# Fine factors built one group earlier in a fused attention and feed-forward kernel on one core

## The chip, the core and the metric

The kernel runs on one core of a Trainium2 chip. The time is the device time of one execution in microseconds (us); three executions of the kernel before took 645.56, 646.25 and 647.49 us, so the median is 646.25 us.

The engines go by the names of the profile: PE multiplies matrices (PEld is its loading of weights), DVE is the vector engine, ACT the scalar engine, POOL the third element-wise engine, which in this kernel mostly issues transfers, and SP only issues transfers. Each engine works through its own list of instructions in a fixed order, and an instruction that waits for a semaphore holds everything behind it on that engine.

## The reference, cut to what matters

```python
# q, k, v: (4 batches, 8 heads, 768 positions, 64), lam: one decay per head, blocks of 64
for b in range(nb):
    intra = ((qb @ kb^T) * Dmask) @ vb              # inside the block, decay lam ** distance
    inter = (qb * lam_pow) @ kv_state               # from everything before it
    out[:, :, sl] = intra + inter
    kv_state = lam_block * kv_state + (kb * rev_pow)^T @ vb
x = attn_out.transpose(0, 2, 1, 3).reshape(3072, 512)
h = x @ w_in                                        # 512 -> 2048
g = h - np.tanh(h)
return g @ w_out                                    # 2048 -> 512
```

All of it is float32. The two large products with `w_in` and `w_out` are most of the arithmetic.

## The kernel before, in words

**Groups and stages.** The 3072 rows are worked in six groups of 512 (128 positions of each of the four batches), numbered 0 to 5; `g` is the group. In each group the attention makes a 512 x 512 block of `x` (tiles `xt`), `up` (from L702) multiplies it with `w_in` in four units `u` of 512 columns, `shrink` takes `h - tanh(h)`, and `down` and `down_twice` multiply the result (tiles `g11`, `g12`, `g21`, `g22` and `gS1`, all shown as `g` or `gS`) with `w_out`. While the units and products of group g run, the attention of group g+1 is woven in between by the function `pieces`, whose names `P2`, `P4`, `P5`, `P6` say after which product a part comes.

**Seven products in place of eight.** Every large product is done by a scheme with seven half-size products in place of eight, numbered 1 to 7, with sums of the operands before and sums of the results after. From group 1 on most of the seven are split a second time in the same way (`down_twice`, matmuls of 128 x 128 by 128 x 128 at L1015); before such a product `sums_twice` makes two new tiles `s1`, `s2` on DVE and a sum in place (L983 to L992). `down_twice` takes the seven small products in the order 1, 2, 6, 5, 7, 3, 4: the third of them (product 6) is the first that reads `s2`, the fourth reads `s1`, and the sixth (product 3) reads a tile from which `s2` has been subtracted after the second small product.

**Factors.** The sums of the `w_out` side don't depend on the group. They are made once and kept in DRAM: `factors` holds the first level, `fine` the second. PE reads them as pieces of 256 KB (tile `wb`), which POOL's queue loads into a ring of eight buffers (`piece`, L875 to L900); a buffer is loaded again when PE has read the piece in it. Fine factors are needed for products 3 to 7 from group 1 on and for products 1 and 2 only from group 2 on, since group 1 does those two unsplit (`down`, L950). `fine_factors(n)` (L927 to L940) makes the missing ones for product n: four loads of 256 KB of `factors` into tiles `f2` (L934), then four subtractions on DVE (L938, shown as L973, the line of the helper `hold`), each followed by a store of 256 KB to `fine` (L939). Before the change both sets are made in `later_units` of group 2: set 1 during unit 0 and set 2 during units 1 to 3.

**Shared buffers.** The tiles of `fine_factors`, of `inner_weights` (`ws2`, sums of `w_in` that POOL stores to `fine_in` at L785), of `inner_tokens` and of `sums_twice` all come from one pool with four buffers (tag `sums`), handed out in turn. A new tile takes the oldest buffer and waits until its last reader, a store among them, is done.

**What sets the order.** Where the code calls `keep_in_program_order` (directly, or by `hold` and `tied`) the engine's order is that of the code. The loads and stores of `fine_factors` are of this kind among themselves; `hold` fixes DVE's sums. The loads of pieces, the stores of `inner_weights` and the stores of results are placed by the framework's scheduler, which decides where they stand on POOL's queue. Two transfers on POOL's queue are never more than eight places apart in flight: each waits for the landing of the eighth before it.

**Group 1 around the change.** `second_units` (L1304) ends with unit 3, `down(1, 1)` in between; `second_products` (L1281) then has `sums_twice` for product 4, the unsplit `down(1, 2)` (matmuls `w`, L950), part P2 of the attention of group 2, and the split product 4 (`y` and `zw`, L1015). `att_end` (L620) ends an attention with the state products of batches 0, 1 (`P0`) and 2, 3 (`P1`), both in the accumulation bank `yb` (L623 and L626).

Of the kernel before, what the change touches and what calls it, by code (L numbers as in the profile page):

```python
# [18 lines left out]
BLK = 128  # L19
# [5 lines left out]
def kernel(  # L25
# [32 lines left out]
    nc = tc.nc  # L58
# [8 lines left out]
    NU = DFF // 512  # L67
# [29 lines left out]
    HF = BLK // 2  # L97
# [12 lines left out]
    def masks():  # L110
        inj = work.tile([128, BLK], F32, name="inj", tag="qd")
        cross = work.tile([128, 4, 2, HF], F32, name="cross", tag="qd")
        lo, hi = ts(0, HF), ts(1, HF)

        for c in range(HF, BLK, 3):
            nc.gpsimd.memset(inj[hi, c:min(c + 3, BLK)], 0.0)
        nc.gpsimd.tensor_copy(inj[hi, 0:HF], ident[hi, HF:BLK])
        for n in range(4):
            tc.keep_in_program_order(nc.vector.tensor_tensor_scan(
                out=cross[hi, n].rearrange("s c i -> s (c i)"), data0=lam_all[hi, n + 4:n + 5].to_broadcast([HF, BLK]),  # L120
                data1=inj[hi], initial=0.0, op0=AL.mult, op1=AL.add))
        m0 = mask0.rearrange("s j p (c i) -> s p j c i", c=2)
        for q in range(2):
            n = ts(q, 2)
            nc.gpsimd.tensor_copy(mask[lo, n, 0:2], m0[lo, q])
            nc.gpsimd.tensor_copy(mask[lo, n, 2], m0[lo, q + 2, :, 0])
            nc.gpsimd.tensor_copy(mask[hi, n, 1], m0[hi, q, :, 1])
        nc.gpsimd.tensor_copy(mask[hi, :, 0:3:2], cross[hi])
# [86 lines left out]
    SUB = (1, 2, 6, 5, 7, 3, 4)  # L215
    GI = 2
    TWICE = (3, 5, 6, 4, 7, 1, 2)
# [364 lines left out]
    def att_state(g, bs, tag):  # L582
        kv = state_products(g, bs, bank("kv", tag, 4 if tag == "att" else 1))
        st = state[:, bs[0]:bs[0] + 2]
        tied(g == 1, nc.vector.tensor_tensor(st, st, kv, op=AL.add))
# [36 lines left out]
    def att_end(g):  # L622

        if g < NG - 1:
            att_state(g, P0, "yb")
            if g + 1 < NG:  # L626
                att_scores(g + 1, P0)
            att_state(g, P1, "yb")

    def att_sums(g, bs=None):  # L630
        x0, x1 = xt[g, 0], xt[g, 1]
# [145 lines left out]
    def inner_weights(u, ns):  # L777
        for n in ns:
            a11, a12, a21, a22 = (a_quarter(n, u, i, k) for i in range(2) for k in range(2))
            t = late["pool"].tile([128, 4, 128], F32, name="ws2", tag="sums", bufs=4)  # L780
            s1, s2, s4 = (t[:, x] for x in range(3))
            for dst, x, y, op in ((s1, a21, a22, AL.add), (s2, s1, a11, AL.subtract), (a21, a11, a21, AL.subtract),
                                  (s4, a12, s2, AL.subtract)):
                tc.keep_in_program_order(nc.vector.tensor_tensor(dst, x, y, op=op))
            nc.gpsimd.dma_start(out=fine_in[INNER.index(n)].rearrange("x p u c -> p u x c")[:, u], in_=t[:, 0:3])  # L785
# [53 lines left out]
    RING = 2 * B  # L839
# [24 lines left out]
    stream = [x for g in range(1, NG) for x in pieces_of(g)]  # L864
    sent = {"n": 0}

    first_blk = next(i for i, x in enumerate(stream) if x[0] == NG - 1)

    def ring(i):
# [3 lines left out]
    def piece(g, n, x):  # L873

        i = stream.index((g, n, x))  # L875
        while sent["n"] < len(stream):
            r = ring(sent["n"])
            mine = [at_ for at_ in range(first_blk if r == "blk" else 0, sent["n"] + 1) if ring(at_) == r]
            if r == "wb" and sum(at_ >= i for at_ in mine) > RING:
                break  # L880
            if r == "blk" and len(mine) % 2 == 1 and len(mine) > 8 and mine[-8] >= i:
                break
            g_, n_, x_ = stream[sent["n"]]
            if r == "wb":
                t = late["pool"].tile([128, 2, 256], F32, name="wb", tag=r, bufs=RING)
            else:
                if len(mine) % 2 == 1:
                    sent["pair"] = late[r].tile([128, 2, 2, 256], F32, name="wb", tag=r)
                t = sent["pair"][:, 1 - len(mine) % 2]
            if isinstance(n_, tuple):  # L890
                nc.gpsimd.dma_start(out=t.rearrange("p m c -> p (m c)"), in_=fine_in[  # L891
                    INNER.index(n_[1]), (5, 6, 3).index(x_)].rearrange("p u c -> p (u c)"))
            elif twice(g_, n_):
                nc.gpsimd.dma_start(out=t.rearrange("p m c -> p (m c)"),  # L894
                                    in_=fine[TWICE.index(n_), SLOT.index(x_)].rearrange("p u c -> p (u c)"))
            else:
                nc.gpsimd.dma_start(out=t, in_=factors[XAT[FACT[n_][1]]][:, 2 * x_:2 * x_ + 2, :])
            blks[stream[sent["n"]]] = t
            sent["n"] += 1
        return blks.pop((g, n, x))  # L900
# [12 lines left out]
    def sums_once(g, dst, x, y):  # L913

        for u in (0, 2):
            tc.keep_in_program_order(nc.vector.tensor_tensor(
                hidden(g, dst)[:, u:u + 2], hidden(g, x)[:, u:u + 2], hidden(g, y)[:, u:u + 2], op=AL.subtract))
# [57 lines left out]
    def sums_twice(g, n, whole=True):  # L975
        a11, a12, a21, a22 = quarter(g, n)
        s1, s2 = (late["pool"].tile([128, NU, 128], F32, name=f"s{x}", tag="sums", bufs=4) for x in (1, 2))
        hold(s1, a21, a22, op=AL.add)
        hold(s2, s1, a11, op=AL.subtract)
        low[g, n] = (s1, s2)  # L980
        if whole:
            sum_third(g, n)
# [75 lines left out]
    def every(product):  # L1058
        for _ in product:
            pass  # L1060

    def steps(product, n):
        for _ in range(n):
            next(product)
# [214 lines left out]
        run(table.get(at_, ()) if g < NG - 1 else ())  # L1279

    def second_products(g):  # L1281
        sums_twice(g, 4)
        sums_once(g, 11, "S1", 11)
        every(down(g, 2))
        pieces(g, "P2")
        pieces(g, "P4")
        sums_twice(g, 5)
        product = down_twice(g, 4)
        steps(product, 4)
        sums_once(g, 21, 21, 11)  # L1290
        sums_twice(g, 6)
        every(product)
        product = down_twice(g, 5)
        steps(product, 2)
        pieces(g, "P5")
        sums_twice(g, 7)
        every(product)
        product = down_twice(g, 6)
        steps(product, 2)
        sums_twice(g, 3)  # L1300
        every(product)
        pieces(g, "P6")
        every(down_twice(g, 7))

    def second_units(g):
        for u in range(NU):
            for n in (2, 6, 5, 7, 1, 4, 3):
                if n != 1:
                    up(g, u, n)
                elif u + 1 < NU:  # L1310
                    up(g, u + 1, 1)
                else:
                    pieces(g, u)
                    inner_weights(u, (1,))
                    every(down(g, 1))
                if u < 2 and n == 5:
                    sums_in(u + 2)
                if (u, n) in ((2, 6), (3, 2)):
                    pieces(g, str(n))
                if n == 7:  # L1320
                    inner_weights(u, (2,))
            inner_weights(u, (1, 5) if u + 1 < NU else (5,))
            if u < 2:
                fine_copies(u + 1)
            if u + 1 < NU:
                pieces(g, u)

    def later_units(g):
        for n in (1, 2):
            made[g, n] = fine_factors(n) if g == GI else iter(())  # L1330
        for u in range(NU):
            if u < 2:
                next(made[g, u + 1], None)
            for n in (3, "begin", 4, "whole", "next", "S") if u == 0 else (3, "whole", 7, "next", "S", 4) if u + 1 < NU else (
                    3, 7, "S", "P4", "cover", 4):
                if n == "begin":
                    begin_unit(g, u + 1)
                elif n == "whole":
                    whole(g, u + 1)
                elif n == "next":  # L1340
                    whole_end(g, u + 1)
                    up(g, u + 1, 6, inside=True)
                elif n == "S":
                    up_sums(g, u)
                elif n == "P4":
                    sums_twice(g, 4)
                elif n == "cover":
                    if twice(g, 1):
                        pieces(g, "P2")
                    else:  # L1350
                        every(down(g, 1))
                else:
                    up(g, u, n, inside=True)
            pieces(g, u)
            if u == 0:
                every(made[g, 1])

    def later_products(g):
        product = down_twice(g, 4)
# [96 lines left out]
```

## Time and profile before

| what | value |
|---|---|
| median of three executions | 646.25 us |
| the profiled execution | 647.1 us, of which 645.3 us are the span from the first to the last instruction |
| PE busy | 636.8 us, 99% of the span, 5894 matmuls |
| DVE busy | 520.6 us, 81% |
| ACT, POOL busy | 234.7 and 234.8 us, 36% each |
| mean transfer rate | 224 GB/s |

The profile comes from one execution, and its times are counted from the first instruction of the span. "Busy" on PE includes the modelled tail of each matmul, so time lost on PE is read from the distance between the starts of matmuls: 112 ns for a 128 x 128 by 128 x 128 one and 216 ns for a 128 x 128 by 128 x 256 one where nothing waits. A wait is put down to the engine or transfer that ended it. The landing time of a transfer is counted from its issue.

### The profile page before, as it was taken

What the parts mean: (1) busy time and instruction counts of PE and PEld (TensorE: products, weight loads), DVE (VectorE), ACT (ScalarE), POOL (GpSimd) and SP (SyncE); (2) the same over time, 40 slices, a digit from 0 to 9 for tenths busy, and PEclk for the clock granted to TensorE, in tenths of its full rate; (3) what the DMA queues carried; (4) which work ended last, traced back from release to release, by engine and by line L of the source; (5) the groups of instructions that cost most, each with busy time, mean ns of one, the idle gap of its engine ahead of it and who ended that gap; (6) DMA issues with size and microseconds to landing.
All of it is one profiled execution on the core that took longest, in us unless ns stands there. A gap on an engine that the chain in (4) does not pass through costs nothing.

```text
span 645.3 us, 15096 instructions
## 1 busy us (share of the span) xinstructions
PE 636.8 (99%) x5894; PEld 589.4 (91%) x5894; DVE 520.6 (81%) x961; ACT 234.7 (36%) x488; POOL 234.8 (36%) x429
## 2 busy tenths in 40 slices
PE   8999999999999999999999999999999999999998
PEld 7888888888888999979999989999988999998997
DVE  5888989987877878799978897878988878467583
ACT  3787883513312123442123344122254222344110
POOL 2001248784323653233655200546301446400440
PEclk9999999999999999999999999999999999999999
DMA  9989988999778877998978975879893586710582
GB/s 201 260 218 200 267 260 285 316 315 301 218 222 230 275 242 231 241 236 254 295 242 293 221 149 122 271 247 307 222 190 99 178 281 222 258 61 1 184 272 68
DMA packets 110006, 144.40 MB, mean 224 GB/s; under 512 B 64304, under 2 KB 81840, under 8 KB 109936
## 3 DMA queue, kind: packets, MB, share of 16 engines
q0 software_dynamic: 31056, 101.47, 49.5%
q1 hardware_dynamic: 78736, 41.96, 28.0%
q8 instruction: 47, 0.77, 0.5%
q14 instruction: 23, 0.19, 0.1%
q10 hardware_dynamic: 144, 0.00, 0.0%
HBM read 120.33 MB, written 24.64 MB: 225 GB/s over the span
## 4 chain that ended last, share of the span: by engine, by line
PE 49%; issue 15%; DVE 9%; POOL 6%; DMA 5%; ACT 1%; SPq 0%; POOLq 0%; DVEq 0%; ACTq 0%
PE y L1015 12%; PE zw L1015 9%; PE y L721 9%; PE y L814 5%; POOL wb L894 4%; PE z L721 3%; DMA q_blk<-in_q_dram 2%; PE z L814 2%; PE y L950 2%; DVE f L325 2%; PE w L814 1%; PE end L1074 1%; PE w L950 1%; DMA f<-factors 1%; PE sp L509 1%
## 5 line engine op out<-in xcount | busy, mean ns | idle before, releaser
L894 POOL DMA_DIRECT2D wb<-fine x217 | 116.7, 539 | 205.4 <-PE y L1015 101.5
L1015 PE MATMUL y<-wb,g 128*128 128x128 f32 x624 | 81.1, 276 | 1.0 <-DMA wb<-fine 0.5
L1018 ACT ACTIVATE q<-y 128x128 f32<-128x128 f32 x108 | 29.9, 277 | 134.9 <-PE y L1015 134.9
L1015 PEld LDWEIGHTS y<-wb,g 128*128 128x128 f32 x624 | 75.2, 192 | 1.9 <-ACT q L1018 0.7
L1015 PE MATMUL zw<-wb,g 128*128 128x128 f32 x416 | 55.0, 275 | 0.0
L1015 PEld LDWEIGHTS zw<-wb,g 128*128 128x128 f32 x416 | 50.6, 192 | 0.0
L721 PE MATMUL y<-xt,w 128*128 128x256 f32 x200 | 46.9, 380 | 0.0
L1098 PE MATMUL h<-xt,w 128*128 128x256 f32 x192 | 44.0, 382 | 0.0
L689 ACT ACTIVATE th<-g 128x512 f32<-128x512 f32 x42 | 26.5, 630 | 46.8 <-DVE g L744 18.6
L721 PEld LDWEIGHTS y<-xt,w 128*128 128x128 f32 x200 | 37.6, 190 | 5.1 <-ACT g L753 0.2
L696 DVE TENSOR_TENSOR g<-g,th 128x512 f32<-128x512 f32 x42 | 29.2, 694 | 15.8 <-ACT th L689 15.4
L721 PE MATMUL z<-xt,ws 128*128 128x256 f32 x168 | 40.4, 381 | 0.0
L1098 PEld LDWEIGHTS h<-xt,w 128*128 128x128 f32 x192 | 35.6, 190 | 5.3 <-DVE w L346 0.5
L721 PE MATMUL y<-tt,w 128*128 128x256 f32 x160 | 38.4, 383 | 1.3 <-DVE g L735 1.0
L721 PE MATMUL y<-tt,ws 128*128 128x256 f32 x160 | 38.2, 380 | 0.2 <-ACT y L672 0.2
L721 PEld LDWEIGHTS z<-xt,ws 128*128 128x128 f32 x168 | 31.6, 190 | 4.7 <-ACT z L672 0.4
L721 PEld LDWEIGHTS y<-tt,w 128*128 128x128 f32 x160 | 29.8, 190 | 6.6 <-DVE g L735 2.0
L721 PEld LDWEIGHTS y<-tt,ws 128*128 128x128 f32 x160 | 29.9, 190 | 4.5 <-ACT y L672 0.6
L1015 PE MATMUL y<-wb,s 128*128 128x128 f32 x248 | 32.8, 275 | 0.0
L1015 PE MATMUL zw<-wb,s 128*128 128x128 f32 x248 | 32.8, 275 | 0.0
L891 POOL DMA_DIRECT2D wb<-fine_in x36 | 19.4, 541 | 30.2 <-DMA v_nat<-in_v_dram 10.4
L1015 PEld LDWEIGHTS y<-wb,s 128*128 128x128 f32 x248 | 30.2, 192 | 0.1
(228 smaller groups left out, 1427.4 us busy)
## 6 DMA issues: line engine op xcount, KB each, us to landing
wb<-fine POOLq DMA_DIRECT2D x217, 256.0 KB, 3.8
wb<-fine_in POOLq DMA_DIRECT2D x36, 256.0 KB, 4.4
fine<-f POOLq DMA_DIRECT2D x24, 256.0 KB, 5.0
raw<-in_moe_w_out_dram POOLq DMA_DIRECT2D x10, 512.0 KB, 5.4
q_blk<-in_q_dram SPq DMA_DIRECT2D x32, 128.0 KB, 5.3
wb<-factors POOLq DMA_DIRECT2D x16, 256.0 KB, 5.5
k_blk<-in_k_dram SPq DMA_DIRECT2D x32, 128.0 KB, 5.0
raw<-in_moe_w_in_dram SPq DMA_DIRECT2D x7, 512.0 KB, 6.7
```

Source lines behind the costliest of these rows:

```text
L325: tc.keep_in_program_order(nc.vector.tensor_tensor(dst[x], a[:, lo:hi], dst[b] if isinstance(b, int) else b[:, lo:hi], op=AL.subtract))
L509: tied(True, nc.tensor.matmul(out=dst, lhsT=keys(p, j, late_), rhs=qt[ts(j, 64), p, rows], start=True, stop=True))
L689: tied(g == 0, nc.scalar.activation(th, src, AF.Tanh))
L696: tied(g == 0 or g >= GI and inside, nc.vector.tensor_tensor(hidden(g, c)[:, u], src, th, op=AL.subtract))
L721: tied(g == 0, nc.tensor.matmul(out=t[:, m, :], lhsT=wt[:, kt, ts(m, 128)], rhs=x[:, kt, :], start=first and m == 0 and kt == 0, stop=kt = ...
L814: tied(True, nc.tensor.matmul(out=dst[:, ts(u, 128)], lhsT=a, rhs=b, start=x in (1, 2, 5) and u == 0, stop=True, skip_group_check=True))
L891: nc.gpsimd.dma_start(out=t.rearrange("p m c -> p (m c)"), in_=fine_in[INNER.index(n_[1]), (5, 6, 3).index(x_)].rearrange("p u c -> p (u c)"))
L894: nc.gpsimd.dma_start(out=t.rearrange("p m c -> p (m c)"), in_=fine[TWICE.index(n_), SLOT.index(x_)].rearrange("p u c -> p (u c)"))
L950: nc.tensor.matmul(out=t[:, m, :], lhsT=a[:, u, kt, ts(m, 128)], rhs=wb[:, kt, :], start=first and u == 0 and m == 0 and kt == 0, stop=u = ...
L1015: tied(True, nc.tensor.matmul(out=dst, lhsT=a[:, u, :], rhs=wb[:, ts(u, 128)], start=x in begins and u == 0, stop=u == NU - 1, skip_group_ ...
L1018: nc.scalar.activation(keep, dst, AF.Copy)
L1098: tied(u == 0 or u == 2 and cs[0] == 11, nc.tensor.matmul(out=hm[c][:, m, :], lhsT=w1[u][:, i, a, ts(m, 128)], rhs=xt[0, t][:, i, :], star ...
```

## The change

There are four edits.

1. Set 1 of the fine factors is made in group 1. In unit 3, right after `inner_weights(3, (1,))`, `fine_factors(1)` is begun, which issues its four loads; after the first of four parts of `down(1, 2)` its subtractions and stores follow, ahead of `sums_twice(1, 4)`, which in turn moves behind the first part of `sums_once`. The third call of `inner_weights` for unit 3, (5), moves ahead to stand with (2). `later_units` of group 2 keeps set 2 alone.
2. The state products of `P1` go to bank `z` in place of `yb`.
3. For groups 2 and 3, the first eight fine pieces of the group's `down_twice` products, which are sent ahead while the units run, are each loaded by two transfers of 128 KB in place of one of 256 KB.
4. One `memset` of 64 columns replaces 22 of at most three columns in `masks`.

```diff
-        for c in range(HF, BLK, 3):
-            nc.gpsimd.memset(inj[hi, c:min(c + 3, BLK)], 0.0)
+        nc.gpsimd.memset(inj[hi, HF:BLK], 0.0)
...
-            att_state(g, P1, "yb")
+            att_state(g, P1, "z")
...
+    halved = [stream.index((g, 4, SUB[0])) + i for g in (GI, GI + 1) for i in range(RING)]
...
-                nc.gpsimd.dma_start(out=t.rearrange("p m c -> p (m c)"),
-                                    in_=fine[TWICE.index(n_), SLOT.index(x_)].rearrange("p u c -> p (u c)"))
+                src = fine[TWICE.index(n_), SLOT.index(x_)].rearrange("p u c -> p (u c)")
+                flat, parts = t.rearrange("p m c -> p (m c)"), 2 if sent["n"] in halved else 1
+                for part in range(parts):
+                    cols = ts(part, 512 // parts)
+                    nc.gpsimd.dma_start(out=flat[:, cols], in_=src[:, cols])
...
     def second_products(g):
+        sums_once(g, 11, "S1", 11)
+        product = down(g, 2)
+        steps(product, 1)
+        every(made[GI, 1])
         sums_twice(g, 4)
-        sums_once(g, 11, "S1", 11)
-        every(down(g, 2))
+        every(product)
         pieces(g, "P2")
...
                     pieces(g, u)
                     inner_weights(u, (1,))
+                    made[GI, 1] = fine_factors(1)
+                    next(made[GI, 1])
                     every(down(g, 1))
...
                 if n == 7:
-                    inner_weights(u, (2,))
-            inner_weights(u, (1, 5) if u + 1 < NU else (5,))
+                    inner_weights(u, (2,) if u + 1 < NU else (2, 5))
+            if u + 1 < NU:
+                inner_weights(u, (1, 5))
...
     def later_units(g):
-        for n in (1, 2):
-            made[g, n] = fine_factors(n) if g == GI else iter(())
+        made[g, 2] = fine_factors(2) if g == GI else iter(())
         for u in range(NU):
-            if u < 2:
-                next(made[g, u + 1], None)
+            if u == 1:
+                next(made[g, 2], None)
...
             pieces(g, u)
-            if u == 0:
-                every(made[g, 1])
```

## The prediction

> **What bounds the kernel now.** I read the page first, then the list of PE's waits, the busy times of chosen stretches, and last the time line around the places that the diff touches.
>
> ```profile
> span 645.3 us, 15096 instructions
> PE 636.8 (99%) x5894; PEld 589.4 (91%) x5894; DVE 520.6 (81%) x961; ACT 234.7 (36%) x488; POOL 234.8 (36%) x429
> ```
>
> PE is the bound, and PE's list stays what it is but for a few neighbours that change places. So the change can only move the short times in which PE waits. In all of the middle there are about 4 us of them, and those that touch this change stand in group 2's units:
>
> ```profile
> PE y L721 <- DVE g L735: 1.0, 2, 0.6
> PE op L573 <- ACT probe L549: 0.4, 1, 0.4
> PE y L721 <- ACT y L672: 0.2, 1, 0.2
> 268.60:297.90 29.30, 27.73 (x271) 23.38 (x265) 27.88 (x44) 12.16 (x22) 7.41 (x12) 1.00 1.02 247
> 372.30:399.00 26.70, 26.70 (x271) 23.50 (x267) 24.10 (x38) 12.12 (x22) 0.00 (x0) 1.00 0.70 152
> ```
>
> The first three lines are PE's waits between 268 and 298 us (total, count, longest). The last two are busy times of the units of groups 2 and 3: length, then PE, PEld, DVE, ACT, POOL, each with its count. Both hold the same 271 matmuls, but group 2 needs 29.3 us and group 3 26.7. Group 2 has both sets of fine factors on DVE; that makes DVE late, and PE waits for it: 2.6 us in all. This is what the change can win.
>
> What it puts at risk is the start of group 1's first split product. DVE, PE and POOL there:
>
> ```profile
> 202.94 0.68 DVE L973 TENSOR_TENSOR s<-g 128x512 f32<-128x512 f32 x1
> 203.65 0.69 DVE L973 TENSOR_TENSOR s<-s,g 128x512 f32<-128x512 f32 x1
> ...
> 207.62 1.16 PE L1015 MATMUL y<-wb,g 128*128 128x128 f32 x8
> 208.61 1.06 PE L1015 MATMUL zw<-wb,g 128*128 128x128 f32 x8
> 209.51 1.06 PE L1015 MATMUL y<-wb,s 128*128 128x128 f32 x8
> ...
> 202.34 0.54 POOL L894 DMA_DIRECT2D wb<-fine  x1 [1.19 <-PE w L950]
> 202.87 1.52 POOL L785 DMA_DIRECT2D fine_in<-ws  x2
> 204.38 0.57 POOL L894 DMA_DIRECT2D wb<-fine  x1
> 204.95 0.71 POOL L906 DMA_DIRECT2D out_dram<-o  x1
> ```
>
> `s2` is ready at 204.3 us and PE wants it at 209.5. The piece at 204.38 can't go sooner: its buffer is read by the last matmul of `down(1, 2)`, which ends at 203.8.
>
> **The moved set, step by step.** POOL's queue as the changed program is built (an order, without times):
>
> ```
> wb     the eighth piece, waits for PE's end of down(1, 2)
> fine_in<-ws2   unit 3's sums for product 1
> f2<-factors x4   the fourth waits for the landing of that fine_in, whose buffer it takes
> out_dram<-o11
> fine<-f2 x4
> wb ...
> ```
>
> On DVE the four subtractions stand ahead of `s1` and `s2`, and these take the buffers of the first two f2 tiles, so `s2` also waits for the landing of the second store. All other instructions of DVE are queued behind, PE's third small product waits for `s2`, and POOL's next pieces for the stores. In times of the profiled execution:
>
> - The eighth piece goes 0.29 us after the matmul's end, as all pieces do, at 204.07, and takes 0.54. The store to `fine_in` takes 0.75, until 205.4; its sums are pushed back by one half of `sums_once` (1.22) and end about 204.5, so say 204.8 to 205.55. Three loads of 0.75 follow, to 207.8.
> - The store must land. Its twelve rows before give 2.5, median 3.6, at most 5.8 us. Transfers issued at 202.8 by SP run until 208.4, so I take 3.9: 208.7. The fourth load is issued then.
> - Its landing has no row at this place. Its eight rows in group 2 give 6.5 to 8.8 us at a DMA share over 1.0, SP's loads beside it. Here SP issues nothing from 203.3 to 252.8 and POOL's pieces are held back, so I take the nearest quiet row, copies of the same `factors` in the same 512-byte runs at 175 us (L924: 3.7, median 4.5, 5.1): 4.5, so 213.2. Ends 3.7 and 8.8.
> - The second subtraction, 0.69; 0.29 to the store's issue; landing 2.6 to 5.8 by its rows, 3.2 by the median of the pieces between 200 and 215 us: 217.4. `s2` takes 0.69, and PE starts at 218.1 in place of 209.5: **8.6 us lost**. All ends low and no wait for the store to `fine_in`: 211.5, 215.1, stall 6.3. All high: stall 17.4.
>
> **What follows the stall.** After `s2` DVE still has the in-place sum, four masks, three sums for product 5 and the subtraction that the sixth small product reads: 0.6 + 4 x 0.47 + 0.6 + 0.7 + 0.6 + 0.7, which is 5.0 us, where PE reaches that product after three small ones of 0.89, at 2.7. So PE waits 2.3 us again. PE's clock comes on top or instead:
>
> ```profile
> 1.07 4.21 PE L369 MATMUL idle<-nothing 128*128 128x128 f32 x18 [1.07 <-DVE nothing L91]
> 644.10:645.30 1.20, 0.00 (x0) 0.00 (x0) 0.00 (x0) 0.00 (x0) 0.00 (x0) 0.51 0.00 0
> ```
>
> At the start 18 matmuls come 213 ns apart, not 112, and go on so until 5.8 us; two us after the last matmul the granted clock reads 0.51. An idle of 8.6 us should bring this back: 4.8 us at half speed lose 2.4 us of work. The two overlap, since slow small products reach the sixth at 5.1 instead of 2.7 us. I count **2.4 us** once; ends 0 (DVE's masks fall into the wait after all, and the clock stays) and 4.7 (both in full). The Trainium skill, TensorE: Matmul & The Clock Gate, Part 1: The HAM clock gate, has the array at half rate after an idle window of about 3.4 us and back after about 3.4 us of work. No row shows an idle that long in mid-run; by it the loss would be 1.7, DVE's 2.3 would decide, and the sum would be 0.1 smaller.
>
> **What group 2 gains.** The distances of matmul starts over the normal step are 0.56 us at 280.6, 0.40 at 285.6, 0.75 at 288.7 and about 0.4 at 296.6, with some 0.1 for the restart after each. The first three hang on DVE, which before them does the four subtractions of set 1 (275.7 to 278.6) and waits 0.5 for a load of set 2, issued late because set 1 held the buffers. I take these three, **2.1 us**; the last comes after a subtraction of set 2, which stays. Ends 0.5 and 2.6.
>
> **Edits that I cost at nothing.** Bank `z` for P1: PE never waited for the two state sums in `yb`; ACT's seed of `y` waited 3.3 us three times and still ended 0.7 us ahead of PE. Now the seed of `z` waits. Ends: 0.4 either way, the size of a single PE wait. Eight more issues in each of two groups, 0.54 each: POOL then sits idle 36 us in group 3, and set 2's loads, 4.3 us later at worst, are wanted some 8 us after landing. If that cover went, 0.5 us as at 287.7. PE also lost 0.7 us at 410.5 to a late piece, which may go or stay: 0.7 either way. The memsets: `ident` is ready at 2.1 us and PE's first use waits until 4.95 for q: 0 both ways, unless q came 3 us sooner.
>
> **Sum.** 8.6 + 2.4 - 2.1 = 8.9. The profiled execution took 647.1 us (span 645.3 and 1.8 around it), which gives 656.0; it lies 0.85 above the median, so against the median: 646.25 + 8.9 = **655.2 us**.
>
> **Rivals.**
> - *Transfers as slow as in group 2.* The fourth load lands after 7.1, the store after 4.6: stall 12.6, sum 12.9, 659.2 us. For: all eight rows of the load are that long. Against: SP's queue is empty here.
> - *Transfers as quick as the shortest.* Store 2.5, loads 3.7, store 2.6 leave a stall of 6.3, and with group 2's full gain 646.25 + 6.3 + 2.4 - 2.6 = 652.4. For: the quiet stretch. Against: three loads are in flight ahead of the fourth. The Trainium skill, DMA: Bandwidth & Descriptors, Anatomy of one DMA, gives 2.0 us plus the bytes at 436 GB/s, 2.6 us for each 256 KB; by it my estimate of the stall is 5.2 and of the time 651.8. No load of this kind came near it in this trace.
> - *The early set holds, and the kernel is faster.* Place: PE's third small product in group 1. DVE idles 3.9 us before 195.9 and POOL 4.6 before 198.9, room for the set. If the loads went there, `s2` would stand in time and only the gain stay: 644.1 us. It decides once `s2` is ready before 211.6, a wait smaller than the gain. Against: the built queue has the loads behind the eighth piece, and even the quickest chain ends at 215.8.
> - *The set 2 that stays keeps group 2 as slow as before*, gain 0.5: 656.8, inside the range.
>
> **How the numbers follow.** Forecast 0.50, slow transfers 0.25, quick ones 0.16, the faster case 0.06, a wash 0.03. No change can be told from one under 0.3%, about 1.9 us: slower 0.91, same 0.03, faster 0.06. The low end, 651.0, lies under the quick case by the open 0.7 at 410.5 and more; the high end, 661.0, over the slow case by 1.8, the part of the all-high chain that I allow. That leaves out the faster and the same case and some 0.08 above.
>
> **What would show it.** In the changed profile: four `f` loads on POOL right behind a piece at about 204 us; PE idle 6 to 13 us before `y<-wb,s` of group 1, ended by DVE `s`, which waits for `fine<-f`; four `f` subtractions on DVE between 211 and 216; a second PE wait or a granted clock near 0.5 just after; group 2's units in 26.7 to 28.8 us. I am wrong if the loads are issued before 199 us, or if PE finds `s2` ready.

## The result

Four executions of the changed kernel took 654.28 to 655.58 us, median **655.22 us**; four of the kernel before, on the same chip, 645.56 to 647.49, median 646.37. The ratio is 1.0133, with a 95% interval of 1.0114 to 1.0152: slower by 1.3%. The forecast was 655.2 us.

The profiled execution took 655.49 us with a span of 653.4. The head of its page:

```profile
span 653.4 us, 15085 instructions
PE 637.0 (98%) x5894; PEld 590.2 (90%) x5894; DVE 520.5 (80%) x961; ACT 234.2 (36%) x488; POOL 242.8 (37%) x424
```

PE does the same work as before (637.0 against 636.8 us busy, 5894 matmuls); 8.1 us of span are added in which it does nothing or runs at half speed. From the list of PE's waits, those of group 1 and later (total, count, longest):

```profile
PE y L1019 <- issue: 8.8, 1, 8.8
...
PE zw L1019 <- DVE g L977: 0.4, 1, 0.4
PE y L719 <- DVE g L733: 0.4, 1, 0.4
```

One wait of 8.8 us carries the loss. The view puts it down to "issue", that is, to nothing it can name; the time line names it. POOL, DVE and PE there:

```profile
204.75 0.54 POOL L899 DMA_DIRECT2D wb<-fine  x1 [1.19 <-PE w L954]
205.46 0.76 POOL L783 DMA_DIRECT2D fine_in<-ws  x1 [0.17 <-issue]
206.20 2.26 POOL L938 DMA_DIRECT2D f<-factors  x3
210.08 0.75 POOL L938 DMA_DIRECT2D f<-factors  x1 [1.62 <-DMA fine_in<-ws]
...
215.96 0.55 POOL L943 DMA_DIRECT2D fine<-f  x1 [1.05 <-DVE f L977]
213.35 0.69 DVE L977 TENSOR_TENSOR f<-f,f 128x512 f32<-128x512 f32 x1 [8.18 <-DMA f<-factors]
214.97 2.15 DVE L977 TENSOR_TENSOR f<-f,f 128x512 f32<-128x512 f32 x3 [0.93 <-DMA f<-factors]
...
218.39 0.69 DVE L977 TENSOR_TENSOR s<-s,g 128x512 f32<-128x512 f32 x1 [0.67 <-DMA fine<-f]
...
223.38 0.68 DVE L977 TENSOR_TENSOR g<-g,s 128x512 f32<-128x512 f32 x1
209.30 1.06 PE L1019 MATMUL zw<-wb,g 128*128 128x128 f32 x8
219.18 2.05 PE L1019 MATMUL y<-wb,s 128*128 128x128 f32 x8 [8.82 <-issue]
...
224.12 1.16 PE L1019 MATMUL zw<-wb,g 128*128 128x128 f32 x8 [0.42 <-DVE g L977]
```

From above: POOL issues the eighth piece, the store to `fine_in`, three loads at once, and the fourth only when that store has landed. DVE then stands idle for 8.18 us until a load lands, 0.93 us for the fourth load and 0.67 us for the second store to `fine`, whose buffer `s2` takes. `s2` ends at 219.08 and PE starts at 219.18. From there eight matmuls take 2.05 us, where those at 209.30 took 1.06: PE runs at half speed (the granted clock, the share of its full speed that PE is allowed, reads 0.5), and then waits once more, for the subtraction at 223.38.

The stretches where the change acts, as busy times (length, PE, PEld, DVE, ACT, POOL with counts, granted clock, mean busy share of the DMA engines, GB/s). First the kernel before: from product 4 of group 1 to the attention's matmuls after its product 6, and from group 2's units to the same place in group 2.

```profile
207.47:226.59 19.12, 19.12 (x187) 18.93 (x178) 17.20 (x29) 4.14 (x13) 10.80 (x20) 1.00 0.83 273
267.43:325.60 58.17, 56.60 (x576) 51.84 (x568) 54.34 (x86) 18.43 (x42) 22.41 (x40) 1.00 0.95 261
```

The same two stretches after, and two short pieces of the first, before and after PE's restart:

```profile
208.16:238.63 30.47, 21.23 (x187) 20.69 (x179) 21.76 (x36) 4.13 (x13) 14.69 (x27) 0.89 0.72 237
278.76:334.98 56.22, 55.83 (x576) 51.92 (x567) 51.86 (x82) 18.87 (x43) 17.19 (x32) 1.00 0.83 238
...
215.70:219.20 3.50, 0.02 (x1) 0.05 (x1) 2.80 (x5) 0.00 (x0) 2.70 (x5) 0.50 0.64 235
219.20:222.50 3.30, 3.30 (x15) 3.30 (x16) 3.27 (x7) 0.28 (x1) 0.54 (x1) 0.50 0.61 199
```

Group 1's stretch holds 187 matmuls both times and grew from 19.12 to 30.47 us: **11.35 lost**. Group 2's fell from 58.17 to 56.22: **1.95 won**. The rest of the 8.1 us of span are waits of 0.4 to 0.8 us: one at 134 us that the trace before has not, and those at 242.7, 410.5 and 475.9 us that the trace after has not. The experiments' traces have such waits at other places, whichever edits are in.

### The profile page after: what moved, and what is told of

Its sections match the earlier page's. It is cut to its first block, busy times and chain, and to the rows that moved or that the text cites. A ratio compares the mean times of both kernels' runs of the same rounds, so it can differ in the third digit from the quotient of the medians.

```text
span 653.4 us, 15085 instructions
## 1 busy us (share of the span) xinstructions
PE 637.0 (98%) x5894; PEld 590.2 (90%) x5894; DVE 520.5 (80%) x961; ACT 234.2 (36%) x488; POOL 242.8 (37%) x424
## 4 chain that ended last, share of the span: by engine, by line
PE 77%; DVE 8%; issue 6%; DMA 5%; POOL 2%; ACT 1%; SPq 0%; DVEq 0%; POOLq 0%; ACTq 0%
PE y L1019 17%; PE y L719 14%; PE zw L1019 12%; PE y L812 7%; PE h L1102 5%; PE z L719 5%; PE z L812 3%; DMA k_nat<-in_k_dram 2%; DMA fine<-f 2%; PE sp L507 2%; PE w L812 2%; PE op L557 1%; PE op L543 1%; PE kv L466 1%; PE end L1078 1%
## 5 line engine op out<-in xcount | busy, mean ns | idle before, releaser
L899 POOL DMA_DIRECT2D wb<-fine x233 | 125.1, 539 | 198.4 <-PE y L1019 98.0
L1019 PEld LDWEIGHTS zw<-wb,s 128*128 128x128 f32 x248 | 31.0, 196 | 0.0
```

The costliest lines, as they stand in the source:

```text
L899: nc.gpsimd.dma_start(out=flat[:, cols], in_=src[:, cols])
L1019: tied(True, nc.tensor.matmul(out=dst, lhsT=a[:, u, :], rhs=wb[:, ts(u, 128)], start=x in begins and u == 0, stop=u == NU - 1, skip_group_ ...
```

## The experiments

The theory: the loss is made by the place of the set (set 1 of the fine factors) in three queues. On POOL its loads stand behind the eighth piece and the store to `fine_in`; in the pool `sums` its tiles share buffers with that store and with `s2`; on DVE its subtractions stand ahead of everything product 4 needs. What follows the stall, half clock and DVE's queue, overlaps and counts once. The rivals: the other three edits share in it; the transfers' own time sets it; the half clock is a loss of its own; DVE's extra work costs group 1 what it saves group 2.

The column "stretch" is the length of group 1's stretch in the profiled execution, "lost" that less 19.12, and "half speed" the time that PE worked at a granted clock of 0.5 inside it.

| kernel | median us | ratio to before, 95% | stretch | lost | half speed |
|---|---|---|---|---|---|
| changed | 655.22 | 1.0114 to 1.0152 | 30.47 | 11.35 | 3.37 |
| e1, edit 1 alone | 655.78 | 1.0128 to 1.0158 | 30.29 | 11.17 | 5.24 |
| e2, all but edit 1 | 645.57 | 0.9981 to 0.9999 | 19.12 | 0.00 | 0 |
| e3, own buffers | 653.22 | 1.0095 to 1.0121 | 27.58 | 8.46 | 5.62 |
| e4, own buffers, spread | 643.20 | 0.9940 to 0.9964 | 19.12 | 0.00 | 0 |
| e5, PE kept busy 16 us | 662.75 | 1.0214 to 1.0287 | 35.21 | 16.09 | 0 |
| e6, other order on DVE | 655.01 | 1.0102 to 1.0152 | 30.45 | 11.33 | 5.97 |
| e7, both | 662.24 | 1.0217 to 1.0265 | 35.21 | 16.09 | 0 |
| e8, long runs | 656.35 | 1.0125 to 1.0189 | 29.94 | 10.82 | 4.17 |
| e9, PE kept busy 8 us | 655.26 | 1.0124 to 1.0150 | 30.04 | 10.92 | 0 |
| e10, that and e6's order | 655.31 | 1.0123 to 1.0156 | 29.93 | 10.81 | 0 |
| e11, sums first | 652.66 | 1.0081 to 1.0111 | 28.47 | 9.35 | 4.23 |
| e12, spread more | 644.15 | 0.9958 to 0.9980 | 19.55 | 0.43 | 0 |

### Which edit it is: e1 and e2

e1 is the kernel before with edit 1 alone; e2 is the changed kernel with edit 1 taken back:

```diff
-                    made[GI, 1] = fine_factors(1)
-                    next(made[GI, 1])
                     every(down(g, 1))
...
-        made[g, 2] = fine_factors(2) if g == GI else iter(())
+        for n in (1, 2):
+            made[g, n] = fine_factors(n) if g == GI else iter(())
...
+            if u == 0:
+                every(made[g, 1])
```

> Edit 1 alone on the kernel before (the set in group 1; P1's state products in yb, whole pieces and the 22 memsets stay). Theory: edit 1 is the whole loss, and the three other edits are worth nothing: 655.2 us within 0.8, PE idle about 9 before y<-wb,s of group 1, then 2.3 more up to the sixth small product. Rival A: the other edits carry part of the loss, so that edit 1 alone gives 653 or less. Rival B: the other edits gave something back (the waits at 242.7, 410.5 and 475.9 us of the trace before, 0.67 + 0.68 + 0.44 = 1.8 us, are gone in the trace after): then about 657.0.

> The changed kernel without edit 1 (bank z for P1, the halved pieces and the one memset stay; both sets of fine factors in group 2 as before). Theory: 646.4 us within 0.7, no PE wait over 0.7 between 205 and 230, group 2's units still near 29.3 us. Rival A (part of the loss): 648 or more. Rival B (they gave back 1.8): about 644.6, with the waits at 242.7, 410.5 and 475.9 gone here too.

Edit 1 alone is slower by 1.43% and loses 11.17 us in the stretch; without it the stretch is 19.12 again. The two stretches in e2:

```profile
207.92:227.04 19.12, 19.12 (x187) 18.93 (x179) 17.19 (x29) 4.14 (x13) 10.80 (x20) 1.00 0.87 278
267.17:325.39 58.22, 56.95 (x575) 51.98 (x567) 54.32 (x86) 18.89 (x43) 22.77 (x41) 1.00 0.99 261
```

Its group 2 takes 58.22 us as before (58.17), while e1's takes 56.06: the gain in group 2 belongs to edit 1 as well. Of the other three edits there is left at most 0.2%: e2 is 0.7 us faster by the medians, and its interval ends just under 1. Rival A falls. Of rival B little is left: e1 took 655.78 us and not 657.0, and e2's 645.57 is 0.1 below the range of the theory, where the rival had 644.6. The waits at 242.7 and 410.5 are gone in e2 and, without any of the three edits, in e1 as well, while e1 has one of 1.3 us at 483.8 and e2 one of 0.8 at 474.9. So no one edit has to be credited with them; as no kernel has two traces, it isn't shown whether such waits change from one execution to the next or with any change to the program. The same holds for the wait at 134 us, 0.4 to 0.75 us long in six of the fourteen traces.

### Which queue it is: e3, e11 and e8

e3 gives the set's tiles buffers of their own, in tiles that are free by then:

```diff
+        if n == 1:
+            three = xpool.tile([128, 3, 2, HB], F32, name="f2", tag="tt")
+            fourth = work.tile([128, 2, HB], F32, name="f2", tag="th")
...
-                t.append(late["pool"].tile([128, NU, 128], F32, name="f2", tag="sums", bufs=4))
+                t.append(own(len(t)) if n == 1 else late["pool"].tile([128, NU, 128], F32, name="f2", tag="sums", bufs=4))
```

> The changed kernel with buffers of their own for the set's four tiles (three in the tile tt, which PE has read by 196, one in th), so that s1, s2, the sums of unit 3 and the fourth load no longer wait for each other's buffers. The built order keeps the four loads right behind the store to fine_in, but both now stand ahead of the eighth piece, and on DVE unit 3's sums stand four instructions earlier; the subtractions stay ahead of s1 and s2. Theory (the stall is a chain of shared buffers, the place on POOL's queue and the order on DVE): the loads go at 201.5 to 203.8 in place of 206.2 to 210.1, land 4.5 to 6.3 later, s2 is ready at 212 to 213.7 in place of 219.1: PE idles 1.8 to 3.5 in place of 9.0, the clock stays up, the wait of 2.3 for DVE's queue behind s2 stays; 648.0 to 649.7 us. Rival: the transfers' own time sets it (three loads of 6.2 in a row), buffers or not: 653.5 to 655.

It took 653.22 us, 3.5 more than the theory's end and close to the rival. POOL and DVE in its time line:

```profile
202.59 0.54 POOL L899 DMA_DIRECT2D wb<-fine  x1 [1.19 <-PE w L961]
...
203.87 2.99 POOL L945 DMA_DIRECT2D f<-factors  x4
...
209.51 0.69 DVE L984 TENSOR_TENSOR f<-f 128x512 f32<-128x512 f32 x1 [4.09 <-DMA f<-factors]
211.89 1.42 DVE L984 TENSOR_TENSOR f<-f 128x512 f32<-128x512 f32 x2 [1.69 <-DMA f<-factors]
```

The mechanism did what was said: the four loads go back to back and neither the fourth load nor `s2` waits for a store. But the loads left at 203.87, not at 201.5, for they now stood behind the seventh piece, which waits for PE until 202.31, and they landed 4.6 to 5.7 us after issue. I had looked past one waiting piece and taken the next for the obstacle. DVE idles 5.8 us in place of 9.8, PE 5.5 in place of 8.8, and then works 5.62 us at half speed. Measured from product 4's start the loads leave 1.9 us sooner than in the changed kernel; that and the buffers together are worth 2.9 of the 11.35 us lost, although the half clock cost 1.1 us more here (5.62 us of it in place of 3.37). The rest is DVE's wait for the loads, the set's own work and what follows.

e11 is e3 with `s1`, `s2` and the sum in place ahead of the set on DVE (the diff is against e3):

```diff
         steps(product, 1)
-        every(made[GI, 1])
         sums_twice(g, 4)
+        every(made[GI, 1])
         every(product)
```

> Buffers of their own for the set's tiles, and s1, s2 and the sum in place of product 4 ahead of the four subtractions on DVE (in e3 they stand behind them). The order of POOL's queue stays as in e3. Theory (it is the wait on DVE that costs, whoever stands behind it): s2 is ready at about 207 and PE's third small product starts on time, but DVE still waits for the loads (until 209.4 and 211.8 in e3) and has the set, four masks and three sums ahead of the subtraction that the sixth small product reads: ready at about 218.5, where PE gets to it at 212.3, a wait of about 6 at zw<-wb,g and the half clock after it: 653 within 1, no better than e3. Rival (only the order of s2 and the set matters): no wait over 1, 645 to 647.

As the theory has it. The wait has moved, as the list of PE's waits in that place shows:

```profile
PE zw L1026 <- DVE g L984: 7.1, 1, 7.1
```

and DVE's time line says why:

```profile
205.60 0.69 DVE L984 TENSOR_TENSOR s<-s,g 128x512 f32<-128x512 f32 x1
...
212.63 1.42 DVE L984 TENSOR_TENSOR f<-f 128x512 f32<-128x512 f32 x2 [2.23 <-DMA f<-factors]
...
218.48 0.68 DVE L984 TENSOR_TENSOR g<-g,s 128x512 f32<-128x512 f32 x1
```

`s2` stands at 206.3 and PE's third small product starts on time, but the subtraction for the sixth still comes after the set, four masks and three sums. PE waits 7.1 us there in place of 5.5 at the third, and the time is 652.66 us, 0.6 from e3. (Its stretch is 0.9 us longer than e3's, whose trace has a wait of 1.1 us at 251.4 that this one has not.) What costs is that DVE's queue stands still, not which of its instructions PE meets first.

e8 reads 2,048 bytes in a row from each partition in place of four times 512:

```diff
+                src = f[:, :, i, ts(j, 128)] if n == 2 else factors[XAT[FACT[n][1]]].rearrange(
+                    "p (x u) c -> p x (u c)", x=4)[:, 2 * i + j].rearrange("p (u c) -> p u c", c=128)
```

> The changed kernel whose four loads of the set read 2,048 bytes in a row from each partition in place of four times 512 (other numbers of the same factors, so that product 1 from group 2 on is computed with the wrong fine factors). The loads took 6.2, 6.2, 6.3 and 4.8 us from issue to landing. Theory: most of that is the queue of transfers issued ahead (the eighth piece, the store to fine_in, SP's four at 203.4 to 205.1), not the short runs: landings within 0.7 us of those, stall 8.3 to 9.0, 654.5 to 655.5. Rival (the short runs are slow): each lands 1.5 us or more sooner, stall 7.5 or less, 653.7 or less.

The first three loads landed 5.9 to 6.1 us after issue and the fourth 3.9. The changed kernel had 6.2 to 6.3 and 4.8, and e1, which has the short runs too, 5.9 to 6.0 and 4.3. The short runs make the issue longer (0.75 us against 0.54), and the landing of the first three by 0.3 at most. The fourth came 0.9 sooner than in the changed kernel, more than the 0.7 expected, but the traces show another difference there. A transfer counts its semaphore up in sixteen steps. In the changed kernel the last step of each of the four loads comes 1.4 to 1.5 us after the fifteenth; in e8 it comes 1.3 after it for the first three and 0.14 for the fourth. So one late step of sixteen makes part of the landing time, and what holds it up is not shown. That the rest comes from transfers issued ahead is what is left, and was not tried by itself. The time, 656.35 us, lies above what either side expected; the stretch (29.94) does not, and this trace has waits of 1.5 us at 484.2 and of 0.4 at 418.4 and 422.4, of the kind that differs from trace to trace.

### What follows the stall: e5, e6, e7, e9 and e10

PE is kept at work inside the stall, in columns of the bank that nothing reads:

```diff
             if x == 2:
                 hold(a12, a12, s2, op=AL.subtract)
+                for _ in range(72 if (g, n) == (GI - 1, 4) else 0):
+                    tied(True, nc.tensor.matmul(out=free, lhsT=ident, rhs=ident, start=False, stop=True,
+                                                skip_group_check=True))
```

> The changed kernel with 72 matmuls of 128x128 on the identity, into free columns of the same bank, after the second small product of group 1's product 4: work for 8.1 us inside the stall of 9.0, so that PE is never idle for long. What it asks: are the half clock and the wait for DVE's queue two losses or one counted twice? Theory (as the prediction counted, once): the clock stays 1.0, PE reaches the sixth small product 2.7 after its restart, and now waits 2.3 there for DVE, in place of 0.6: 655.2 within 0.5. Rival: the half clock (1.7 in the trace after, 2.6 in that of edit 1 alone) is a loss of its own: 653.0 to 653.6.

e6 moves the three sums for product 5 behind the subtraction that the sixth small product reads, and e7 does both:

```diff
-        sums_twice(g, 5)
         product = down_twice(g, 4)
-        steps(product, 4)
+        steps(product, 2)
+        sums_twice(g, 5)
+        steps(product, 2)
```

> The changed kernel with the three sums for product 5 moved behind the subtraction that product 4's sixth small product reads: DVE has that ready 2.0 us sooner (about 222.0 in place of 224.1). Theory: with the clock at half, PE gets there at 223.5, so the second wait of 0.6 goes and the half clock alone is left, 1.7 to 3.4 according to where the return of the clock falls: 654.6 to 656. Rival (DVE's queue is the loss): 653.

> Both of these edits. Theory: the follow-up of 2.3 is the larger of two overlapping waits, so only both edits together remove it: PE reaches the sixth small product at 221.9, DVE is ready at 222.1: a wait of about 0.3 left, 653.2 us within 0.5, about 2 less than either edit alone. Rival (the losses add): each alone already wins its part, and together no more than their sum.

e5 and e7 missed their mark: each of these matmuls is two entries of 112 ns on PE, so 72 of them were 16.1 us of work, not 8.1, and PE itself became what product 4 waited for. They still say one thing: the stretch is 35.21 us in both, 16.09 over 19.12, which is the added work and nothing more (the other 2.8 us by which e5 is slower than the changed kernel have their likely place in waits of 1.3 and 1.6 us that its trace shows in group 2). Once DVE has had 16 us and the clock has not fallen, nothing follows. e6 is as expected: no second wait, 5.97 us of work at half speed (3.0 lost), and 11.33 lost in all, as in the changed kernel. e9 and e10 repeat e5 and e7 with 36:

```diff
-                for _ in range(72 if (g, n) == (GI - 1, 4) else 0):
+                for _ in range(36 if (g, n) == (GI - 1, 4) else 0):
```

> The changed kernel with 36 matmuls on the identity in the stall (each is two entries of 112 ns on PE, so that 72 of them were 16.1 us of work; 36 are 8.06). As the one with 72 before it: are the half clock and DVE's queue two losses or one counted twice? Theory: once; the clock stays 1.0 and PE now waits about 2.3 at the sixth small product, where the trace after has 0.6: 655.2 within 0.6. Rival: the half clock (1.7 in the trace after, 2.6 to 3.0 in those of edit 1 alone and of the other order on DVE) is a loss of its own: 652.3 to 653.5.

> 36 matmuls on the identity in the stall and the three sums for product 5 behind the subtraction for the sixth small product. Theory: PE gets to the sixth small product 2.7 after its restart, DVE has its tile 3.0 after: 0.3 left of a follow-up of 2.3 to 3.0: 653.0 within 0.6. Rival (something else than these two follows the stall): 655.

e9 bears the theory out. The clock stays at 1.0 and the time does not change (655.26 against 655.22), since PE now waits longer for DVE at the sixth small product. PE's waits in this place:

```profile
PE zw L1019 <- DVE g L977: 2.0, 1, 2.0
PE y L1019 <- DVE s L977: 0.3, 1, 0.3
```

In e10 the theory fails. Both waits should have gone, and 653.0 us was expected; it took 655.31. PE's waits there:

```profile
PE zw L1019 <- DVE gS L977: 1.1, 1, 1.1
PE y L1019 <- DVE s L977: 0.8, 1, 0.8
```

The wait at product 4's sixth small product is down to 0.3 us (too short for this list), and a new one of 1.1 us stands at the sixth of *product 5*, where the tile is `gS`. DVE's subtraction for it, before and in e10:

```profile
216.91 0.68 DVE L973 TENSOR_TENSOR gS<-gS,s 128x512 f32<-128x512 f32 x1
...
228.69 0.68 DVE L977 TENSOR_TENSOR gS<-gS,s 128x512 f32<-128x512 f32 x1
```

In the kernel before, DVE works without a gap of more than 0.3 us from 202.9 to 221.6 us, so a delay ahead of this stretch reaches all of it. There its subtraction for product 5 ends 10.1 us after the start of the stretch at 207.47, and PE asks for it 0.85 later; in e10 it ends 21.6 after the start of its stretch. A delay of 11.5 with a margin of 0.85 is a loss of 10.65 us at that place, whatever is mended before it; the stretch of e10 lost 10.81. So there are three limits within 0.6 us of each other: DVE's whole delay (10.8 in e10), DVE at product 4 (10.9 in e9) and the half clock (11.3 in e6 and in the changed kernel). Removing any one uncovers the next.

### The set where DVE has room: e4 and e12

e4 has e3's buffers, `s1` and `s2` of product 4 with nothing of the set ahead of them, and the four subtractions later (the diff shows the order alone):

```diff
         steps(product, 1)
-        every(made[GI, 1])
         sums_twice(g, 4)
...
         sums_twice(g, 7)
         every(product)
+        steps(made[GI, 1], 2)
         product = down_twice(g, 6)
         steps(product, 2)
+        every(made[GI, 1])
         sums_twice(g, 3)
```

> As the kernel with buffers of their own, and the four subtractions moved: two after product 5 of group 1 and two after the second small product of product 6, where DVE has gaps (0.6, 0.2, 0.2, 0.6, 1.0 us between 221 and 230 in the trace before); s1 and s2 of product 4 stand as before the change. Theory: no wait at product 4, the gain in group 2 stays: 655.2 - 11.3 = 643.9, at most 644.8; faster than before by 0.25 to 0.4 per cent. Rival: 2.8 us more of DVE in group 1 cost PE about as much there as they saved in group 2, wherever they stand: 646 to 647.

It took 643.20 us, ratio 0.9952 (0.9940 to 0.9964): faster than both kernels, a little better than expected. Its two stretches:

```profile
207.29:226.41 19.12, 19.12 (x187) 18.93 (x179) 18.65 (x31) 4.14 (x13) 12.19 (x23) 1.00 0.90 298
268.08:324.26 56.18, 55.83 (x575) 51.91 (x568) 51.84 (x82) 18.89 (x43) 17.19 (x32) 1.00 0.86 239
```

Nothing is lost in group 1 up to product 6, and group 2's gain of 2.0 us stays, so the last rival, that DVE's work costs as much in group 1 as it saved, falls. One new wait shows in product 7 of group 1:

```profile
PE zw L1026 <- DMA wb<-fine: 1.3, 1, 1.3
```

e12 sets the four stores further apart, one subtraction each after products 4 and 5, in the middle of product 6 and after it (the diff is against e4):

```diff
         sums_twice(g, 6)
         every(product)
+        steps(made[GI, 1], 1)
         product = down_twice(g, 5)
...
-        steps(made[GI, 1], 2)
+        steps(made[GI, 1], 1)
         product = down_twice(g, 6)
         steps(product, 2)
-        every(made[GI, 1])
+        steps(made[GI, 1], 1)
         sums_twice(g, 3)
         every(product)
+        every(made[GI, 1])
```

> As e4, with one subtraction each after products 4 and 5, in the middle of product 6 and after it, so that the four stores to fine do not go between 222 and 225.5 us all at once. e4 had one new wait: 1.4 us at 231.8 for a piece that was issued at 225.48 and landed 7.8 later, behind those stores, where pieces alone keep the DMA engines at 0.9. Theory: with the stores apart this wait goes, 641.8 to 642.5. Rival (the ring of eight pieces runs dry there however the stores stand): 643.2 as e4. Or DVE is late for product 5's sixth small product by the one subtraction moved ahead of it: up to 0.7 back.

The wait for the piece is gone, 0.43 us come back in the stretch, and from product 4 to group 2's units e12 takes 59.7 us against e4's 60.8. The medians don't show it: e12 took 644.15 us, where 641.8 to 642.5 was expected, and its ratio is 0.9969 (0.9958 to 0.9980) against e4's 0.9952, with the span of both profiled executions at 642.6. The interval of the one just reaches into the other's, and e12's trace has 0.6 us at 134 and 0.5 at 473.6, so it stays open which of the two is the better. Both beat the kernel before.

## Why the prediction was right

**The chain on POOL and DVE.** It was right link by link, though not in every size. Product 4 begins 0.69 us later in the trace after, so that much is taken off each time. The eighth piece goes at 204.06 (forecast 204.07), the store to `fine_in` at 204.8 (204.8). That store lands after 4.34 us (3.9), the fourth load after 4.77 (4.5), the second store to `fine` after 2.33 (3.2), and PE starts at 218.5 (218.1). The stall is 8.99 us where 8.6 was forecast. The store to `fine` was sized 0.9 too long, the other two landings 0.7 too short together, and three gaps of 0.1 to 0.3 between a landing and the next start were left out. One premise did not hold: SP's queue was not empty here. Four of its loads went at 203.4 to 204.7 us and had landed by 209.6, ahead of the set's loads. The first two of these took 6.2 and 6.3 us, so that the first subtraction ended at 214.04, only 0.8 us before the fourth load landed: the chain nearly hung on loads that the forecast had left out of it.

**That `s2` waits for a store** was right (0.67 us of DVE), and e3 prices the shared buffers, together with loads that leave 1.9 us sooner, at 2.9 us. What the prediction did not see is that DVE's idle time itself, 9.8 us with 2.9 of added work, would cost about the same whatever PE met first (e11).

**The follow-up, 2.4 us.** Measured 1.69 for the half clock and 0.58 for the second wait, 2.27 together. That the two overlap and count once is shown by e9. Its terms were off. The 4.8 us at half speed, read from the start of the execution, was 3.37 in this trace and 4.2 to 6.0 in five others. DVE's list behind `s2` was forecast at 5.0 us (its terms add up to 5.1) and took 4.98. And behind DVE's 2.3 at product 4 stood a third limit of the same size at product 5, which only e10 brought out. The Trainium skill, TensorE: Matmul & The Clock Gate, Part 1: The HAM clock gate, has a budget of about 3.4 us until the full rate is back, from which the prediction's second estimate, 1.7 for the clock, was worked out. This trace agrees with 3.37 us at half speed and 1.69 lost, but that is the least that the runs show, not the usual.

**Group 2's gain, 2.1 us.** Measured 1.95 here, 2.0 to 2.1 in e1 and e4. Right in size, less so by name: of the four waits the last, which I let stay, is gone, and one of 0.55 us stays at 297.1, in the place of one that I had counted as won.

**The edits costed at nothing** came to 0.7 us by e2's median, with an interval that ends just short of nothing. The 0.7 us at 410.5 that the prediction left open is gone in e1 and in e2, so it hangs on no one edit.

**The sum.** That the forecast meets the median so closely is partly luck. The three terms as measured make 9.3 us (8.99 + 2.27 - 1.95), 0.4 over the forecast's 8.9; the other waits of the trace, which no term held, are 1.3 us shorter than before and take that back and more.

**The rivals.** Slow transfers would have given 659.2 and quick ones 652.4; the fourth load took 4.8 us, between their 7.1 and 3.7. No load of the set comes under 3.8 in any trace, and none of its stores under 2.3. The Trainium skill, DMA: Bandwidth & Descriptors, Anatomy of one DMA, gives an estimate of 2.6 us for a transfer of this size. For a load behind others that is too short here; the changed kernel's four stores, with little ahead of them, took 2.3 to 3.0, which agrees. The case in which the early set holds did not come about, but its price was near: 644.1 was forecast for it, and e4, where `s2` stands in time, takes 643.2.

## What to carry to other kernels

Work moved to an earlier place takes its waits with it: on an engine with a fixed order, the price of a moved instruction is the time that the queue stands still, to be set against the smallest margin of *everything* behind it up to the engine's next gap, here three limits within 0.6 us of each other. Look first at which buffers the moved tiles share and what stands ahead of their loads, and put the instruction that waits where the engine has gaps; the same four subtractions cost 11.35 us at one place, and in e4, some 8 us later, PE waits for none of them, but 1.4 us for a piece behind their stores. And before an overlap is mended at one end, ask which limit comes next: mending the clock, the order on DVE, and then both, won nothing.

## What the runs showed of the hardware

**The half clock comes in whole periods of 3.41 us.** Times from the records of the granted clock, in six traces with a long idle time:

| kernel | PE's last matmul ends | clock falls to 0.5 | PE starts again | clock back at 1.0 | length at 0.5 |
|---|---|---|---|---|---|
| changed | 210.36 | 215.72 | 219.18 | 222.55 | 6.83 |
| e1 | 209.60 | 213.03 | 218.03 | 223.27 | 10.24 |
| e3 | 209.92 | 214.26 | 215.46 | 221.08 | 6.82 |
| e6 | 210.13 | 214.11 | 218.38 | 224.35 | 10.24 |
| e8 | 209.57 | 211.79 | 217.86 | 222.03 | 10.24 |
| e11 | 212.14 | 216.63 | 219.22 | 223.45 | 6.82 |

The length is two or three times 3.41 us, and the time at full clock ahead of it is a whole number of such periods too (211.63 us or 62 of them in the changed kernel, from 4.10 us on), while the fall comes 2.2 to 5.4 us after the last matmul and the return 3.4 to 6.0 after the restart. This fits periods that run on by themselves, of which one without much work (at most 35%, in e8) brings the clock down and one nearly full of work brings it back: counted back from the return in steps of 3.41, a period that PE filled to 75% was not enough in e6, and one filled to 99% was in the changed kernel. The Trainium skill, TensorE: Matmul & The Clock Gate, Part 1: The HAM clock gate, has a free-running window of 3.4 us, which agrees. So an idle time of 5.5 to 9 us cost another 1.7 to 3.0 us in these six traces by chance of where it fell, and 2.0 us of idle time in e9 cost nothing.

**Pieces alone nearly fill the DMA engines.** In the split products PE reads a piece of 256 KB every 0.89 us, and between 222 and 228 us the kernel before has the DMA engines busy 0.88 to 0.92 with that alone. In e4 four stores of 256 KB issued between 222.3 and 225.5 were enough: the four pieces issued behind them landed 8.0 us after issue (median), where those from 212 to 224 us took 3.3 to 4.5, and the ring of eight ran dry. In e12, with the stores further apart, that wait is gone.

**A wait can lose its name.** PE's longest wait in the changed kernel was listed as "issue"; in e9, where the same wait came after other matmuls and was short, the list gives DVE's `s`. The time line shows `s2` ending 0.1 us before PE starts, and that is what names it.
